# Batch 0's first stage in two tiles, filters released on half of x, and the last V/G weights behind D's first slab

## The chip, the cores and the metric

One NeuronCore of a Trainium2 chip runs the whole kernel. The metric is the device time of one execution in microseconds (us), median of several. Each kernel's time is compared with runs of the kernel before on its own chip and of its own rounds. Each trace is one execution, and most of the traces compared come from different chips. Times inside an execution count from the start of its span.

## The reference

```python
def _attn_ref(x, filt_r, filt_i):                    # x: 8 x 3008 x 256, f32
    X = np.fft.rfft(x, axis=1)
    Y = X * (filt_r + 1j * filt_i)[None]             # 1505 frequencies x 256
    return np.fft.irfft(Y, n=x.shape[1], axis=1)

def _moe_ref(x, w_gate, w_val, w_out):               # 24064 tokens, 256 -> 1536 -> 256
    return (np.maximum(x @ w_gate, 0.0) * (x @ w_val)) @ w_out
```

The kernel computes the second of the first. 3008 = 94 x 32, so the Fourier transform is done in stages: A (along the 94), B (forward along the 32, times the filter, and back), C (back along the 94, into y transposed), then the V, G and O matmuls on blocks of 512 tokens.

## The kernel before

Only batch 0 is exposed. The other seven batches' stages run between V/G/O matmuls. What follows is the start, cut to what the change touches; "..." marks cuts.

```python
XF = [pro.tile([128, NX2 * D], FP32, name=f"XF{c}") for c in range(N2 // NX2)]   # x, two halves
AS = pro.tile([128, NC2, N2 // NC2, D], BF16)        # stage A of batch 0
AT = pro.tile([128, 32, D], BF16)                    # the same, turned in 32 x 32 blocks
...
def first_a(p, s, h):                                # 16 of these; h is half of D
    ...
    nc.tensor.matmul(psA, WA[:, 0:128], xf[:, n:n + 4, h * D // 2:(h + 1) * D // 2], ...)
    nc.scalar.copy(AS[:, 4 * s:4 * s + 4, p, h * D // 2:(h + 1) * D // 2], psA)

def turn_a(h):
    src = AS.rearrange("p l c d -> p (l c) d").bitcast(FP32).rearrange("p n d -> p d n")
    dst = AT.bitcast(FP32).rearrange("p k d -> p d k")
    cols = slice(h * D // 4, (h + 1) * D // 4)
    nc.vector.transpose(dst[:, cols, :], src[:, cols, :])
...
load_own_filters()
hold_gpsimd(XF[1][:, 2 * q - 8:2 * q])     # GpSimd waits here for three quarters of x,
for _ in filters:                          # then issues the rest of the filters
    pass
...                                        # stage A on PE; filler matmuls; turns
place_filter(1, 1, 0, nc.scalar.copy)      # rows of the filters doubled: by ACT, by DVE,
place_filter(1, 0, 0, nc.vector.tensor_copy)
for half in range(2):                      # and by DMAs on SP's queue,
    for a in range(2):
        place_filter(0, a, half, nc.sync.dma_start)
load_x(1, nc.sync, ...)                    # behind which stands batch 1's x
...
def first_b(amid):
    for i in range(6):
        fwd(0, i)                          # PE: psX
        if i > 1:
            inv(0, i - 2, cuts=cuts)       # PE: psD; ACT: dsb; SP: Dbuf<-dsb
        for e in range(2):                 # DVE, or ACT copy + GpSimd, times the filters
            product(0, i, e, 0)
            product(0, i, e, 1, pool=(i, e) in POOL_U)
        amid(i)                            # stage A matmuls of batch 1 in between
...
def amid(i):
    ...
    if i in (2, 4):                        # third and fourth quarter of V and G
        load_vg((i + 2) // 2 * DFF // 4, (i + 4) // 2 * DFF // 4)
    for _ in range((1, 1, 1, 2, 1, 2, 1)[i]):
        next(early)()
hold_gpsimd(AT[0:32, NG - 1, D - 8:])
load_vg(0, DFF // 2)
first_b(amid)
load_d(0, 0, 2)                            # first two slabs of D, read on SP's queue
for i, f in enumerate(early):              # rest of batch 1's stage A
    f()
    if i == 5:
        item_c(0, 0); item_c(0, 1)         # PE: psY <- D, then yT
hold_gpsimd(yTs[0][:, 0, 0:8])
load_o()                                   # W_out
```

The engines in the profile: PE is TensorE (matmuls; PEld are its weight loads), DVE is VectorE, ACT is ScalarE, POOL is GpSimd, and SP is SyncE, which here only issues DMAs. An eviction copies a result out of PSUM, a turn is the transpose of one half of stage A in 32 x 32 blocks, a hold is a small copy that makes GpSimd wait for a tile, and a slab is a piece of D that is read back for stage C.

The names in the profile: `XF` (x), `psA` (stage A's result), `psX` (the forward transform), `Ftr`/`Fti` (the filters' real and imaginary parts), `psY` (stage C's result), `AS`, `AT`, `tt`/`uu` (products), `psD`/`dsb` (stage B's result and its eviction), `Dbuf` (D in HBM), `dC` (a slab of D read back), `asb`/`Abuf`/`at` (the same way for batch 1's stage A), `WvT`/`WgT`/`WoT` (weights).

Of the kernel before, what the change touches and what calls it, by code (L numbers as in the profile page):

```python
# [12 lines left out]
FP32 = mybir.dt.float32  # L13
BF16 = mybir.dt.bfloat16
# [15 lines left out]
N1, N2 = 94, 32  # L30
# [5 lines left out]
def _ap(t, offset_elems, ap_list):  # L36
    return dataclasses.replace(
        t, offset=t.offset + offset_elems, ap=[list(p) for p in ap_list]
    )
# [81 lines left out]
def kernel(  # L121
# [10 lines left out]
    nc = tc.nc  # L132
    B, S_, D = x.shape
    DFF = moe_w_gate.shape[1]
    NFT = DFF // 128
    assert S_ == S and D == 256 and DFF % 128 == 0
    NC2 = 8
# [14 lines left out]
    pro = prologue.enter_context(tc.tile_pool(name="pro", bufs=1))  # L152
# [3 lines left out]

    XF = [pro.tile([128, NX2 * D], FP32, name=f"XF{c}") for c in range(N2 // NX2)]
    WA = pro.tile([128, 128 + NROW], FP32)
    AS = pro.tile([128, NC2, N2 // NC2, D], BF16)
    AT = pro.tile([128, 32, D], BF16)  # L160
    WF = consts.tile([128, 4, 32], FP32)
    M1 = consts.tile([NROW, N1], BF16)
# [65 lines left out]
    def load_own_filters():  # L228
        for src, dst in FILT:
            nc.gpsimd.dma_start(dst[64:95:2, NG - 2:, :],  # L230
                                _ap(src, 47 * D, [[N1 * D, 16], [-47 * D, 2], [1, D]]))
            nyq.append(pro.tile([1, D], BF16, tag="nyq", bufs=2, name="nyq"))
            nc.gpsimd.dma_start(nyq[-1], _ap(src, (S // 2) * D, [[D, 1], [1, D]]))
# [8 lines left out]
    def place_nyq():  # L242
        for (src, dst), n in zip(FILT, nyq):
            nc.vector.tensor_copy(dst[96:97, NG - 1, :], n)

    def load_vg(c0, c1):
        for (w_hbm, w_sb) in ((moe_w_val, WvT), (moe_w_gate, WgT)):
            nc.gpsimd.dma_start(w_sb[:, :, c0:c1],
                                _ap(w_hbm, c0, [[DFF, 128], [128 * DFF, 2], [1, c1 - c0]]))
# [7 lines left out]
    def hold_gpsimd(tile_):  # L257

        scr = sb.tile([128, 8], FP32, tag="scr", bufs=2)
        nc.gpsimd.tensor_copy(scr[:tile_.shape[0]], tile_)  # L260
# [4 lines left out]
    def fft_tag(side=False):  # L265
        if side and turn.get("side"):
            return turn["side"]
        turn["i"] += 1
        return turn["tags"][turn["i"] % len(turn["tags"])]

    def first_a(p, s, h):

        psA = ps.tile([128, 4, D // 2], FP32, tag=fft_tag(True), name="psA")
        xf = XF[p // 2].rearrange("p (n d) -> p n d", d=D)
        n = p % 2 * NC2 + 4 * s
        nc.tensor.matmul(psA, WA[:, 0:128], xf[:, n:n + 4, h * D // 2:(h + 1) * D // 2],
                         start=True, stop=True)
        nc.scalar.copy(AS[:, 4 * s:4 * s + 4, p, h * D // 2:(h + 1) * D // 2], psA)

    def turn_a(h):  # L280

        src = AS.rearrange("p l c d -> p (l c) d").bitcast(FP32).rearrange("p n d -> p d n")
        dst = AT.bitcast(FP32).rearrange("p k d -> p d k")
        cols = slice(h * D // 4, (h + 1) * D // 4)
        nc.vector.transpose(dst[:, cols, :], src[:, cols, :])  # L285
        ats[0] = AT

    def items_a(b):
# [136 lines left out]
    def first_b(amid):  # L425

        cuts = (0, 2, 4, 5, 6)
        for i in range(6):
            fwd(0, i)
            if i > 1:  # L430
                inv(0, i - 2, cuts=cuts)
            for e in range(2):
                product(0, i, e, 0)
                product(0, i, e, 1, pool=(i, e) in POOL_U)
            amid(i)
        inv(0, 4, cuts=cuts)
        amid(6)
        inv(0, 5, cuts=cuts)

    dCs = {}  # L440

    def load_d(b, z0=0, z1=NZ):
        for z in range(z0, z1):
            dC = sb.tile([NROW, 8, D], BF16, tag="dC", bufs=6)
            for e in range(2):
                nc.sync.dma_start(dC[48 * e:48 * e + 48],
                                  _ap(Dbuf[b], (64 * e + 16 * z) * NG * D,
                                      [[D, 48], [48 * D, 8], [1, D]]))
            dCs[b, z] = dC
# [13 lines left out]
    def item_c(k, h):  # L463

        if h == 0:
            yTs[k] = sb.tile([128, 2, W], BF16, tag="yT", bufs=3, name="yT")
        tag = fft_tag() if k == 0 else ("psv", "psg")[h]
        psY = ps.tile([128, W], FP32, tag=tag, name="psY")
        for (o, b, n2, n1, w) in runs(k * W, W):
            nc.tensor.matmul(psY[:, o:o + w],  # L470
                             dCs[b, n2 // 8][:, n2 % 8, h * 128:(h + 1) * 128], M1[:, n1:n1 + w],
                             start=True, stop=True)
        dst = yTs[k][:, h]
        if h == 0:
            nc.scalar.copy(dst, psY)  # L475
        else:
            nc.vector.tensor_copy(dst, psY)
# [63 lines left out]
    q = NX2 * D // 4  # L541
# [13 lines left out]
    for (src, dst) in FILT:  # L555
        nc.vector.memset(dst[64:128, NG - 2:, :], 0.0)
    load_own_filters()
    hold_gpsimd(XF[1][:, 2 * q - 8:2 * q])
    for _ in filters:
        pass  # L560

# [4 lines left out]
    for s in range(2):  # L566
        for h in range(2):
            first_a(0, s, h)
    for i in range(3):
        make_back_u(i)  # L570
    for p, h in ((1, 0), (1, 1), (2, 0), (3, 0), (2, 1), (3, 1)):
        for s in range(2):
            first_a(p, s, h)
    place_own()
    for h in range(2):
        turn_a(h)
# [15 lines left out]
    def amid(i):  # L592
        if i == 3:
            place_nyq()
        if i in (2, 4):
            load_vg((i + 2) // 2 * DFF // 4, (i + 4) // 2 * DFF // 4)
        for _ in range((1, 1, 1, 2, 1, 2, 1)[i]):
            next(early)()

# [3 lines left out]
    first_b(amid)  # L603
    turn["tags"], turn["side"] = ("fft", "psv", "psg", "pso"), None
    load_d(0, 0, 2)
    for i, f in enumerate(early):
        f()
        if i == 5:
            for h in range(2):
                item_c(0, h)  # L610
# [21 lines left out]
    for b in range(1, B):  # L632
# [4 lines left out]
        else:  # L637
            for j, e in enumerate((-74, -69, -62, -55) if b == 2 else (-74, -69, -64, -57)):
                l = (22, 29, 34, 43)[j] if b == 2 else end - 115 + NFT * j
# [11 lines left out]
        for i in range(7):  # L651
            l = -35 + 5 * i if b == 1 else -40 + 6 * i
# [49 lines left out]
```

## Time and profile before

| | us |
|---|---|
| median before the change (first three runs, 896.4 to 898.69) | 896.96 |
| span of the profiled execution | 896.3 |
| first product of stage B starts | 32.82 |
| last eviction of stage B ends | 49.91 |
| D's last write lands | 55.46 |
| first psY of stage C starts | 60.15 |
| first V/G product on DVE | 64.91 |

The page gives busy us, share of the span and instructions of each engine, then the line of what the DMA engines moved in 40 slices of the span:

```profile
PE 874.9 (98%) x7186; PEld 507.2 (57%) x7186; DVE 572.8 (64%) x871; ACT 499.9 (56%) x889; POOL 364.6 (41%) x360
...
GB/s 222 275 242 97 128 134 162 102 109 116 136 150 129 99 126 123 142 138 98 99 161 135 109 102 95 191 124 93 108 141 154 117 32 82 74 82 36 37 29 54
```

PE has next to nothing to win after the start, and the DMA engines are busiest in the first three slices, 67 us. Landing times in this document come from the records of the sixteen completions of each transfer in the trace: a transfer has landed with its last one.

### The profile page before, as it was taken

To read this page: it belongs to the slowest core of one execution; us is meant where nothing else is said; L and a number is where in the kernel's file an instruction comes from. 1 tells how busy PE (TensorE), PEld (TensorE's weight loads), DVE (VectorE), ACT (ScalarE), POOL (GpSimd) and SP (SyncE) were. 2 spreads that over 40 slices of the span, in tenths; PEclk is the share of its full clock that TensorE was granted. 3 is DMA by queue.
4 is the path that set the end of the run, shared out by engine and by line. 5 is a ranking of instruction groups with operands and counts; after the bars stand their busy time and mean duration, and the time that the engine had idled before them with its cause. 6 is when DMAs were issued, how large, how long until landed. Compare 5 with 4: busy or idle time off the path is not lost.

```text
span 896.3 us, 19093 instructions
## 1 busy us (share of the span) xinstructions
PE 874.9 (98%) x7186; PEld 507.2 (57%) x7186; DVE 572.8 (64%) x871; ACT 499.9 (56%) x889; POOL 364.6 (41%) x360
## 2 busy tenths in 40 slices
PE   8779999999999999999999999999999999999998
PEld 3325555566556565566655665556655566666665
DVE  3827765577765776667766677656766577655554
ACT  5545655556555556555655565655555556555553
POOL 4431599028671386515673167811768000000001
PEclk9989999999999999999999999999999999999999
DMA  8994448444465344563365433753346512231111
GB/s 222 275 242 97 128 134 162 102 109 116 136 150 129 99 126 123 142 138 98 99 161 135 109 102 95 191 124 93 108 141 154 117 32 82 74 82 36 37 29 54
DMA packets 110769, 107.26 MB, mean 120 GB/s; under 512 B 20167, under 2 KB 95463, under 8 KB 110038
## 3 DMA queue, kind: packets, MB, share of 16 engines
q1 hardware_dynamic: 86998, 78.20, 34.1%
q0 software_dynamic: 22960, 26.40, 12.4%
q10 hardware_dynamic: 720, 1.45, 0.4%
q8 instruction: 56, 0.92, 0.4%
q14 instruction: 35, 0.29, 0.1%
HBM read 60.42 MB, written 48.23 MB: 121 GB/s over the span
## 4 chain that ended last, share of the span: by engine, by line
PE 90%; DMA 5%; DVE 2%; ACT 1%; SPq 1%; issue 1%; POOL 0%; DVEq 0%; POOLq 0%
PE psV L486 27%; PE psG L486 27%; PE psO L505 26%; PE psF L342 3%; PE psD L413 2%; PE psY L470 2%; PE psX L383 2%; DMA dC<-Dbuf 1%; PE psA L295 1%; DMA at<-Abuf 1%; DMA Ftr<-Ftr 1%; DMA Ftr<-in_filt_r_dram 1%; DMA Dbuf<-dsb 1%; DMA XF<-in_x_dram 1%; DVE AT L285 0%
## 5 line engine op out<-in xcount | busy, mean ns | idle before, releaser
L491 DVE SCALAR_TENSOR_TENSOR prod<-psG,vsb 128x512 bf16<-128x512 f32 x564 | 389.1, 690 | 265.2 <-ACT vsb L489 256.3
L489 ACT CAST vsb<-psV 128x512 bf16<-128x512 f32 x564 | 332.1, 589 | 262.7 <-PE psV L486 205.3
L486 PE MATMUL psV<-yT,WvT 128*128 128x512 bf16 x1128 | 336.9, 380 | 0.5 <-ACT asb L349 0.5
L505 PE MATMUL psO<-WoT,prod 128*128 128x256 bf16 x2256 | 336.4, 273 | 0.0
L486 PE MATMUL psG<-yT,WgT 128*128 128x512 bf16 x1128 | 335.3, 379 | 0.8 <-ACT dsb L420 0.3
L505 PEld LDWEIGHTS <-prod 128*128 128x128 bf16 x2256 | 220.5, 98 | 143.5
L486 PEld LDWEIGHTS <-WgT 128*128 128x128 bf16 x1128 | 110.1, 98 | 136.6 <-issue 3.8
L486 PEld LDWEIGHTS <-WvT 128*128 128x128 bf16 x1128 | 98.7, 98 | 42.0 <-issue 30.6
L260 POOL CAST scr<-prod 128x8 f32<-128x8 bf16 x24 | 4.6, 192 | 259.7 <-DVE prod L491 259.7
L528 POOL DMA_DIRECT2D out_dram<-osb x5 | 2.6, 535 | 195.9 <-ACT osb L518 195.9
L518 ACT COPY osb<-psO 128x512 f32<-128x512 f32 x92 | 53.9, 586 | 27.9 <-PE psO L505 26.8
L399 DVE TENSOR_TENSOR tt<-psX,Ftr 128x512 bf16<-128x512 f32 x96 | 65.2, 682 | 1.6 <-PE psX L383 1.6
L328 POOL TENSOR_TENSOR fold<-XP 128x1024 f32<-128x1024 f32 x24 | 56.6, 2356 | 20.9 <-PE psF L342 19.5
L399 DVE TENSOR_TENSOR uu<-psX,Fti 128x512 bf16<-128x512 f32 x89 | 60.6, 681 | 0.0
L420 ACT CAST dsb<-psD 128x512 bf16<-128x512 f32 x96 | 51.6, 589 | 13.1 <-PE psD L413 13.1
L315 POOL DMA_DIRECT2D XP<-in_x_dram x96 | 56.7, 596 | 3.1 <-PE psY L470 1.5
L329 POOL TENSOR_TENSOR XP<-XP 128x1024 f32<-128x1024 f32 x24 | 56.4, 2350 | 1.9
L470 PE MATMUL psY<-M,dC 96*128 96x94 bf16 (+18 forms) x604 | 38.1, 200 | 8.0 <-DMA dC<-Dbuf 7.8
L475 ACT CAST yT<-psY 128x512 bf16<-128x512 f32 x47 | 27.6, 586 | 30.6 <-PE psY L470 30.4
L349 ACT CAST asb<-psF 128x512 bf16<-128x512 f32 x48 | 25.8, 589 | 30.5 <-PE psF L342 30.5
L349 DVE CAST asb<-psF 128x512 bf16<-128x512 f32 x48 | 30.9, 686 | 18.6 <-PE psF L342 18.6
L470 PEld LDWEIGHTS <-dC 96*128 96x128 bf16 x604 | 34.8, 98 | 12.5 <-issue 8.3
(75 smaller groups left out, 490.4 us busy)
## 6 DMA issues: line engine op xcount, KB each, us to landing
dC<-Dbuf SPq DMA_DIRECT2D x64, 192.0 KB
XP<-in_x_dram POOLq DMA_DIRECT2D x48, 256.0 KB, 6.0
Dbuf<-dsb SPq DMA_DIRECT2D x23, 512.0 KB
at<-Abuf SPq DMA_DIRECT2D x28, 384.0 KB
XP<-in_x_dram POOLq DMA_DIRECT2D x96, 96.0 KB, 2.7
Abuf<-asb SPq DMA_DIRECT2D x96, 96.0 KB
out_dram<-osb SPq DMA_DIRECT2D x69, 94.0 KB
XF<-in_x_dram SPq DMA_DIRECT2D x15, 256.0 KB
```

The lines of the kernel that those rows point to most:

```text
L315: nc.gpsimd.dma_start(xp[r:r + 24, 0:4:2, :], _ap(x, (b * N1 * N2 + o) * D, [[N2 * D, 24], [47 * N2 * D, 2], [1, 512]]))
L328: tt(t, xp[:, 0:2], xp[:, 2:4], op=ALU.add)
L329: tt(xp[:, 2:4], xp[:, 0:2], xp[:, 2:4], op=ALU.subtract)
L349: copy(asf[:, :, q, :], banks[q])
L399: nc.vector.tensor_tensor(p, psX, filt, op=ALU.mult)
L420: nc.scalar.copy(dsb[:, a, o:o + 2, :], psD[a])
L470: nc.tensor.matmul(psY[:, o:o + w], dCs[b, n2 // 8][:, n2 % 8, h * 128:(h + 1) * 128], M1[:, n1:n1 + w], start=True, stop=True)
L486: nc.tensor.matmul(pt[:, :W], w[:, h, ft * 128:(ft + 1) * 128], yt[:, h, :], start=(h == 0), stop=(h == 1))
L489: nc.scalar.copy(vsb, psV[:, :W])
L491: nc.vector.scalar_tensor_tensor(prod, in0=psG[:, :W], scalar=0.0, in1=vsb, op0=ALU.max, op1=ALU.mult)
L505: nc.tensor.matmul(psO[:, t % 2], prods[ft][:, t * 128:(t + 1) * 128], WoT[:, ft, :], start=(ft == 0), stop=(ft == NFT - 1))
L518: copy(osb[:, t0 % 2:t % 2 + 1], psO[:, t0 % 2:t % 2 + 1])
```

## The change

The intent has three parts. Part 1 keeps the two halves of batch 0's stage A in a tile each, so that each half can be turned when its own eight evictions are done. Part 2 lets GpSimd issue the filters when half of x is there, not three quarters. Part 3 takes the last two quarters of V and G (called the quarters below) out of stage B and issues them when D's first slab has landed.

```diff
-    AS = pro.tile([128, NC2, N2 // NC2, D], BF16)
+    AS = [pro.tile([128, NC2, N2 // NC2, D // 2], BF16, name=f"AS{h}") for h in range(2)]
...
-        nc.scalar.copy(AS[:, 4 * s:4 * s + 4, p, h * D // 2:(h + 1) * D // 2], psA)
+        nc.scalar.copy(AS[h][:, 4 * s:4 * s + 4, p, :], psA)
...
-        src = AS.rearrange("p l c d -> p (l c) d").bitcast(FP32).rearrange("p n d -> p d n")
+        src = AS[h].rearrange("p l c d -> p (l c) d").bitcast(FP32).rearrange("p n d -> p d n")
...
-        nc.vector.transpose(dst[:, cols, :], src[:, cols, :])
+        nc.vector.transpose(dst[:, h * D // 4:(h + 1) * D // 4, :], src)
...
-    hold_gpsimd(XF[1][:, 2 * q - 8:2 * q])
+    hold_gpsimd(XF[0][:, 4 * q - 8:4 * q])
...
-        if i in (2, 4):
-            load_vg((i + 2) // 2 * DFF // 4, (i + 4) // 2 * DFF // 4)
...
     load_d(0, 0, 2)
+    hold_gpsimd(dCs[0, 0][:, 7, D - 8:])
+    for c in range(2, 4):
+        load_vg(c * DFF // 4, (c + 1) * DFF // 4)
```

More of the change, by code (lines that the diff above doesn't have):

```diff
@@ L277, in first_a @@
                          start=True, stop=True)
-        nc.scalar.copy(AS[:, 4 * s:4 * s + 4, p, h * D // 2:(h + 1) * D // 2], psA)
+        nc.scalar.copy(AS[h][:, 4 * s:4 * s + 4, p, :], psA)
     def turn_a(h):
-        src = AS.rearrange("p l c d -> p (l c) d").bitcast(FP32).rearrange("p n d -> p d n")
+        src = AS[h].rearrange("p l c d -> p (l c) d").bitcast(FP32).rearrange("p n d -> p d n")
         dst = AT.bitcast(FP32).rearrange("p k d -> p d k")
-        cols = slice(h * D // 4, (h + 1) * D // 4)
-        nc.vector.transpose(dst[:, cols, :], src[:, cols, :])
+        nc.vector.transpose(dst[:, h * D // 4:(h + 1) * D // 4, :], src)
         ats[0] = AT
```

## The prediction

> **What bounds the kernel now.** I read the page first, then the chain of waits, then the timelines of the start, then the DMA queues in stretches of 2 us. The page has PE busy 98% of the span, and the chain that ends last is 90% PE. After about 75 us the chain is an unbroken run of V, G and O matmuls, which the change does not touch. So only what lies before the first V matmul (62.79 us) can move the end, and each us gained there should come off the end. The chain of the start, in order of time (start, length, what):
>
> ```profile
> 27.75 4.06 DVE AT L285
> 31.84 0.96 DVE Fti L240
> 32.84 0.68 DVE tt L399
> ...
> 49.93 5.53 DMA Dbuf<-dsb
> ...
> 59.06 5.86 DMA at<-Abuf
> ```
>
> Three pieces are to be seen: turns of AT ahead of the first product, a 5.5 us wait for D's last write, then reads. The timelines (start, length, engine, line, operation, and in brackets the idle time before it) show why:
>
> ```profile
> 19.51 0.59 ACT L278 CAST AS<-psA 128x512 bf16<-128x512 f32 x1 [0.27 <-PE psA L276]
> ...
> 22.94 0.59 ACT L278 CAST AS<-psA 128x512 bf16<-128x512 f32 x1 [0.27 <-PE psA L276]
> 28.48 2.75 ACT L240 COPY Fti<-Fti 32x3072 bf16<-32x3072 bf16 x1 [4.95 <-DMA Fti<-in_filt_i_dram]
> ```
> ```profile
> 23.56 8.25 DVE L285 STREAM_TRANSPOSE AT<-AS 128x2048 f32<-128x2048 f32 x2 [10.21 <-ACT AS L278]
> 31.84 0.95 DVE L240 COPY Fti<-Fti 32x3072 bf16<-32x3072 bf16 x1
> 32.82 0.69 DVE L399 TENSOR_TENSOR tt<-psX,Ftr 128x512 bf16<-128x512 f32 x1
> ```
> ```profile
> 14.50 0.19 POOL L260 COPY scr<-XF 128x8 f32<-128x8 f32 x1 [6.14 <-DMA XF<-in_x_dram]
> 14.99 0.61 POOL L225 DMA_DIRECT2D Ftr<-in_filt_r_dram  x1 [0.30 <-issue]
> ```
> ```profile
> 60.15 1.01 PE L470 MATMUL psY<-M,dC 96*128 96x94 bf16 x12 [6.08 <-DMA dC<-Dbuf]
> ```
>
> DVE has stood idle 10.21 us when both turns run, and they start only after the sixteenth eviction (22.94 + 0.59). In the program order the last eviction of half 0 is the eighth of the last twelve, the one at 19.51. PE later waits 6.08 us for D's first slab. The stretches (PE, weight loads, DVE, ACT, POOL busy; then granted clock, DMA share, GB/s):
>
> ```profile
> 14.00:16.00 2.00, 2.00 (x6) 0.88 (x5) 0.00 (x0) 1.26 (x3) 1.20 (x3) 1.00 0.56 234
> 30.00:32.00 2.00, 0.14 (x5) 0.14 (x8) 1.97 (x2) 1.23 (x1) 0.12 (x1) 1.00 1.08 368
> 34.00:36.00 2.00, 2.00 (x10) 0.44 (x10) 1.90 (x4) 1.26 (x3) 0.82 (x2) 0.50 1.00 307
> 50.00:52.00 2.00, 2.00 (x6) 0.81 (x5) 0.00 (x0) 1.45 (x3) 0.00 (x0) 1.00 1.17 295
> 60.00:62.00 2.00, 1.85 (x14) 1.31 (x15) 0.69 (x1) 0.59 (x1) 0.58 (x2) 0.50 1.19 260
> ```
>
> DMA is full from 16 to 54 us but for one hole at 14 to 16. The clock is halved after each PE gap.
>
> **What the Trainium skill says.** "DMA: Bandwidth & Descriptors", section "Queues, rings and completion order": each DMA engine takes turns between the queues it has work for, packet by packet. The trace agrees: at 44 to 46 us the hardware queue took 61.4% and the software queue 55.8%. So weights issued by GpSimd delay D's writes. The same page, "Anatomy of one DMA — SWDGE (gpsimd) path", fits a transfer as about 2.0 us plus its bytes; the trace shows 3.6 us at the least from issue to landing of a filter piece and 10.2 us for the last, which queue. "TensorE: Matmul & The Clock Gate", "What's actually happening": a free-running window of 3413 ns, and an idle window halves the clock. The trace agrees: 0.50 at 34 to 36 us after a gap of 3.78 us, and at 58 to 62 us.
>
> **Part 1, two AS tiles.** The instruction order is the same on every engine; only the waits of the two turns differ (each now has its own). Turn 0 can start at 19.51 + 0.59 + 0.03 = 20.13 us. A turn takes 8.25 / 2 = 4.12, so it ends at 24.25. Half 1 is written by 23.53, so turn 1 runs 24.25 to 28.37. Then the DVE filter copy, 0.95, and the first product at 29.36 in place of 32.82: **3.46 us** on the path, if the filters are there.
>
> **Part 2, filters held for half of x.** The first product also needs Ftr's first-half copies (landed 27.59 by the completion records, so no bound on 29.36), and the next one the ACT copy of Fti, which ended at 28.48 + 2.75 = 31.23. Without part 2 that would take back 1.3 us. XF[0] landed at 12.23, the old hold's piece at 14.34: the issue moves 2.11 us earlier, from 14.99 to 12.88. First packets came 1.4 us after the issue, so now at 14.3. x has then about 0.8 us of packets left, which half rate stretches to 1.6, to land near 17.0 in place of 16.17. PE wants that piece at 12.37 + 6 x 0.86 = 17.5, so stage A is not delayed. The filters gain 2.1 less about 0.8 of sharing: 1.3 us. Fti lands at 27.1, and ACT ends at 29.9; the second product wants it at 29.97. Parts 1 and 2 fit within 0.1 us. Batch 1's first x, which landed at 31.19, comes at 29.9, and PE wants it at 28.8: a stall of 1 us that hides beside DVE.
>
> Stage B itself (32.82 to its last eviction at 48.84 + 1.07 = 49.91, 17.1 us) should shrink too. PE's gap before it falls from 3.78 us to 0.3, so the half clock at 33.0 to 36.4 should go; DVE idled 0.70, 0.31 and 0.87 us for PE there. POOL loses four weight issues (0.75, 0.71, 0.75, 0.71) that stood between its products. ACT, busy 13.6 of those 15.2 us from its first copy, is the floor. I take **1.0 us**, a choice, so B's last eviction is at 49.91 - 3.46 - 1.0 = 45.4.
>
> **Part 3, last V/G quarters after D's slab.** It removes 0.79 MB of weights (as written) from beside D's writes. Work on the DMA engines, as share times length of the 2 us stretches by queue: filters 9.4 us, hardware queue to 42 us 14.2, first V/G half 4.5, last quarters 5.4, then D and A writes 7.2 + 1.1. That is 41.8 in the 39 us from 16.4 to 55.4, a capacity of 1.07. Without the last quarters and half of the last A write it is 35.9, so 33.5 us, and from 15.3 (the hole filled) it ends at 48.8. The engines' own path gives 45.4 plus about 4 (the first D slab took 3.1 us from issue to landing with few others about), so 49.4. The two limits are close and will rub; I take 50.0 for D's last write in place of 55.46: **5.5 us**, which contains all of the gains above (3.5 + 1.0 + about 1.0 of a shorter write). The read of the first slab takes 4.5 us as before (55.55 to 60.02), so it lands at D = 54.5.
>
> The cost: the quarters now go behind D. Hold and first issue at D + 0.6, first packets at about D + 2.4. The remaining reads (half of slab 1, A of batch 1) have then some 3.4 us of work; two pieces of c=2 are 2.7 us. Taking turns, they end at D + 7.2 and land by D + 7.7; c=3 lands near D + 10.5; W_out (5 us of work) at D + 13 and D + 16. Before, V started 2.77 us after the slab, reached feature block 6 at D + 8.7, block 9 at D + 11.7, and O at D + 15.8 and 17.1. All have about 1 us to spare. I allow **0.6 us** of stall on average. The half clock after D's wait may give back some: one window rather than two would be worth 0.6, not sure because the window runs free. Sum: 5.5 - 0.6 + 0.4 = **5.3 us**.
>
> **Rivals.** (a) Weights late: the last quarters miss block 6 or 9 by 2 to 4 us, or W_out misses O. For it: earlier quarters took 6.4 to 10.1 us from issue, and 8 us is all there is; against it: the reads beside them end soon. Time 893.5 to 896. (b) Early filters slow x: XF[1] lands after 17.5 and stage A loses up to 2 us, or Fti still lands at 28.4 because DMA is full, so the second product waits on ACT as before. For it: shares of 1.0 to 1.2; against: the idle hole. Time 892.5 to 894. (c) DMA is not what D's write waits for, its own latency is, and the gain is parts 1 and 2 alone: 3.5 us, 893.5. (d) Everything fits and both half-clock windows vanish: 889.
>
> **Range and chances.** 896.96 - 5.3 = **891.7 us**. (a) to (c) pull up, (d) down; runs spread about 1 us. So 889.2 to 895.0. The whole stretch at stake is 62.8 us with at most some 8 us to win, and 2% is 17.9 us: faster by over 2% 0.01, within 2% 0.98, slower 0.01.
>
> **What would show it.** The first turn at 20.1 and first product near 29.4; ACT's Fti copy near 27; clock 1.00 at 29 to 36; D's last write landing near 50 and the first psY near 54.6; no PE gap over 0.5 us in V/G of block 0 (a gap ended by WvT or WgT means rival a). If the first product comes at 29.4 and psY less than 4 us earlier, the DMA sum was wrong. A change that showed only after 75 us would refute the whole reading.

## The result

| | before | changed |
|---|---|---|
| median, us (4 runs each) | 897.83 (896.4 to 899.18) | 891.36 (891.01 to 893.75) |
| ratio | | 0.9934, 95% interval 0.9909 to 0.9959 |
| span of the profiled execution | 896.3 | 889.2 |

A ratio is the mean time of one kernel's fast runs over the mean of the other's of the same rounds, so not quite the ratio of the medians. 1 - 0.9934 is 5.9 us of 897.8. By the 2% mark this is "same", and it is clear of noise.

The timelines of the changed kernel: first DVE, ACT and GpSimd, then PE (start, us, engine, line, operation, and in brackets the idle time before it and what ended it). Lines of the source are one lower than before.

```profile
20.12 8.29 DVE L284 STREAM_TRANSPOSE AT<-AS 128x2048 f32<-128x2048 f32 x2 [6.19 <-ACT AS L278]
28.45 0.95 DVE L240 COPY Fti<-Fti 32x3072 bf16<-32x3072 bf16 x1
29.43 0.69 DVE L398 TENSOR_TENSOR tt<-psX,Ftr 128x512 bf16<-128x512 f32 x1
```
```profile
24.89 2.75 ACT L240 COPY Fti<-Fti 32x3072 bf16<-32x3072 bf16 x1 [1.36 <-DMA Fti<-in_filt_i_dram]
```
```profile
12.01 0.19 POOL L260 COPY scr<-XF 128x8 f32<-128x8 f32 x1 [3.63 <-DMA XF<-in_x_dram]
```
```profile
54.66 0.62 PE L469 MATMUL psY<-M,dC 96*128 96x94 bf16 x12 [3.97 <-DMA dC<-Dbuf]
```

Turn 0 starts at 20.12 in place of 23.56 and the first product at 29.43 in place of 32.82. Stage C's first psY starts at 54.66 in place of 60.15. The chain that ended last, at stage B's end (start, us, what), and the stretches (PE, weight loads, DVE, ACT, POOL busy, clock, DMA share, GB/s):

```profile
45.45 1.07 ACT dsb L419 x2
46.52 0.02 ACT asb L297
46.54 2.43 DMA Dbuf<-dsb
...
49.44 5.09 DMA dC<-Dbuf
```
```profile
32.00:34.00 2.00, 1.06 (x15) 0.59 (x15) 1.71 (x3) 2.00 (x5) 1.98 (x2) 1.00 1.01 353
34.00:36.00 2.00, 1.34 (x17) 0.43 (x19) 1.19 (x2) 1.82 (x4) 1.99 (x3) 1.00 0.95 334
```

D's last write takes 2.43 us where it took 5.53, the slab's read takes longer than before (5.46 us in place of 4.47, by the completions), and the clock is whole at 34 to 36 us. The first V/G product on DVE comes at 59.27, 5.64 us earlier. The distance between the two traces stays 5.64 us, product by product, until block 4. There PE of the kernel before waited once more, 1.8 us for a slab of batch 1's D, and the profiled spans end 7.1 us apart. In the fourteen profiles that wait was 2.0 us in e2, 1.8 in this one, 1.5 in e1 and 0 to 0.5 in the others. All three are kernels with the quarters inside stage B, but two more of that kind (e5, e9) did not have it, so whether the change has a part in it is not shown. What is read below is the 5.64 us of the start.

### The profile page after: what moved, and what is told of

It is laid out like the page before. It is cut to its first block, busy times and chain, and to the rows that moved or that the text cites. A ratio compares the mean times of both kernels' runs of the same rounds, so it can differ in the third digit from the quotient of the medians.

```text
span 889.2 us, 18975 instructions
## 1 busy us (share of the span) xinstructions
PE 866.7 (97%) x7065; PEld 506.8 (57%) x7186; DVE 572.9 (64%) x871; ACT 500.0 (56%) x889; POOL 365.3 (41%) x361
## 4 chain that ended last, share of the span: by engine, by line
PE 86%; DVE 4%; ACT 4%; DMA 3%; issue 2%; POOL 0%; SPq 0%; DVEq 0%; POOLq 0%; ACTq 0%
PE psG L485 27%; PE psO L504 25%; PE psV L485 25%; DVE prod L490 3%; PE psF L341 3%; ACT vsb L488 3%; PE psD L412 2%; PE psX L382 2%; PE psY L469 2%; DMA Ftr<-Ftr 1%; DMA Ftr<-in_filt_r_dram 1%; PE psA L294 1%; DMA dC<-Dbuf 1%; DMA XF<-in_x_dram 1%; ACT dsb L419 0%
## 5 line engine op out<-in xcount | busy, mean ns | idle before, releaser
L485 PE MATMUL psG<-yT,WgT 128*128 128x512 bf16 x1107 | 331.0, 379 | 6.9 <-DVE prod L490 0.8
L485 PE MATMUL psV<-yT,WvT 128*128 128x512 bf16 x1030 | 315.8, 380 | 0.5 <-ACT asb L348 0.5
L517 ACT COPY osb<-psO 128x512 f32<-128x512 f32 x92 | 54.0, 586 | 27.9 <-PE psO L504 26.5
L476 DVE CAST yT<-psY 128x512 bf16<-128x512 f32 x47 | 32.0, 681 | 11.6 <-PE psY L469 11.6
```

Source lines behind the costliest of these rows:

```text
L485: nc.tensor.matmul(pt[:, :W], w[:, h, ft * 128:(ft + 1) * 128], yt[:, h, :], start=(h == 0), stop=(h == 1))
L517: copy(osb[:, t0 % 2:t % 2 + 1], psO[:, t0 % 2:t % 2 + 1])
```

## The experiments

Twelve runs were made, one of them of the changed kernel again, all with correct results (the labels e7 and e10 are not on record). These times (us) are from the profiled execution of each; "PE waits" is PE's wait for batch 1's x inside stage B, "lag" runs from the end of stage B's last eviction to the landing of D's last write, "slab read" from the first read's issue to the landing of the second half of the first slab.

| kernel | Fti copy on ACT starts | first product | PE waits | stage B | last eviction | lag | slab read | first psY |
|---|---|---|---|---|---|---|---|---|
| before | 28.48 | 32.82 | - | 17.09 | 49.91 | 5.55 | 4.47 | 60.15 |
| changed | 24.89 | 29.43 | 0.16 | 17.09 | 46.52 | 2.46 | 5.46 | 54.66 |
| e1_tiles_only | 28.61 | 29.61 | 4.06 | 20.57 | 50.18 | 6.26 | 3.80 | 60.45 |
| e2_hold_only | 25.52 | 32.73 | - | 17.28 | 50.01 | 5.23 | 3.73 | 59.19 |
| e3_weights_only | 26.74 | 32.36 | - | 17.27 | 49.63 | 2.45 | 5.58 | 57.88 |
| e4_old_hold | 27.66 | 29.28 | 3.03 | 20.06 | 49.34 | 2.43 | 5.58 | 57.58 |
| e5_warm_only | 27.79 | 32.52 | - | 17.09 | 49.61 | 5.37 | 3.97 | 59.17 |
| e6_a_write_behind_d | 26.19 | 29.35 | 1.03 | 17.09 | 46.44 | 3.07 | 3.67 | 53.40 |
| e8_copy_first | 25.17 | 29.12 | 0.69 | 20.77 | 49.89 | 2.44 | 5.65 | 58.20 |
| e9_weights_back | 28.57 | 29.60 | 2.06 | 19.14 | 48.74 | 5.42 | 3.69 | 58.06 |
| e11_changed_again | 27.66 | 29.39 | 2.19 | 20.37 | 49.76 | 2.44 | 5.50 | 57.92 |
| e12_both_moved | 24.90 | 29.16 | 0.37 | 17.09 | 46.25 | 2.48 | 3.97 | 52.91 |
| e13_at_behind_w | 26.87 | 29.17 | 1.58 | 17.52 | 46.69 | 2.44 | 5.53 | 54.88 |
| e14_later_item | 25.18 | 29.00 | 0.40 | 17.21 | 46.21 | 2.65 | 3.74 | 52.82 |

Each row is one execution. That of the changed kernel was the fastest of its four; those of e1, e4 and e11 were the slowest of theirs, so rows next to each other differ by luck as well as by edit.

The theory going in: the start is a serial chain, and the total of DMA work bounds D's write. The rival for the second half: D's write follows the engines by a fixed delay.

### One part at a time

**e1_tiles_only**: the kernel before with the AS hunks alone.

```diff
-    AS = pro.tile([128, NC2, N2 // NC2, D], BF16)
+    AS = [pro.tile([128, NC2, N2 // NC2, D // 2], BF16, name=f"AS{h}") for h in range(2)]
...
```

> Only the two stage-A tiles (part 1), added to the kernel before. Theory (serial chain, DMA total bounds D's write): first turn at 20.1 us, first product at 29.4, but the second product waits for the ACT copy of Fti until about 31.3, so stage B's last eviction ends near 47.8 (before 49.9, changed kernel 46.5); D's last write still lands at 54.5 to 55.4 because the same bytes are queued in the DMA engines, so psY gains only 0 to 1 us and the time is 0 to 1 us under before. Rival (D's write follows the engines by a fixed delay): D lands 5.5 us after the last eviction, near 53.3, and the time is about 2.2 us under before.

Ratio 0.9988, interval 0.9954 to 1.0022: no gain shown. The first turn came at 19.72 and the second product at 31.39, as expected. But stage B took 20.57 us, so its last eviction was even later than before. Both theories missed that. PE's timeline shows the wait:

```profile
28.16 0.41 PE L382 MATMUL psX<-AT,F 64*64 64x256 bf16 x8 [0.48 <-DVE AT L284]
32.63 1.39 PE L294 MATMUL psA<-XF,WA 128*96 128x512 f32 x2 [4.06 <-DMA XF<-in_x_dram]
```

PE kept to the program's order: the second forward product started at 34.02 us, behind that matmul. It is a stage A matmul of batch 1, recorded behind the first forward product, and that x is read on SP's queue behind the copies of the filters. Turning earlier alone brings PE to that matmul before its data: SP issued the read that PE waited for at 26.87, where it does so at 23.36 in the changed kernel.

**e2_hold_only**: the kernel before with the hold's hunk alone.

```diff
-    hold_gpsimd(XF[1][:, 2 * q - 8:2 * q])
+    hold_gpsimd(XF[0][:, 4 * q - 8:4 * q])
```

> Only the earlier filter hold (part 2), added to the kernel before. Theory: Fti lands near 25 us in place of 28.4 as in the changed kernel, the first product stays at 32.8 because both turns still wait for the sixteenth eviction, and the last eviction stays at 49.9; the DMA queue is 1 to 2 us ahead, so D's last write may land 1.0 to 1.5 us earlier: gain 0 to 1.5 us. Rival (D's write follows the engines by a fixed delay): no gain at all, 0.0 us.

Fti came at 25.52, and first product and last eviction did not move. D's write landed at 55.24, 0.22 us earlier: the fixed delay, not the DMA total. psY was 0.96 us earlier, all but 0.22 of it from a shorter slab read. The timing was poor (ratio 1.0033, interval 0.998 to 1.0086, one run of 905.37), so no gain and no loss can be claimed.

**e3_weights_only**: the kernel before with part 3's hunks alone.

```diff
-        if i in (2, 4):
-            load_vg((i + 2) // 2 * DFF // 4, (i + 4) // 2 * DFF // 4)
...
+    hold_gpsimd(dCs[0, 0][:, 7, D - 8:])
+    for c in range(2, 4):
+        load_vg(c * DFF // 4, (c + 1) * DFF // 4)
```

> Only the last V/G quarters behind D's first slab (part 3), added to the kernel before. Theory: start unchanged (first product 32.8, last eviction 49.9), D's last write lands some 2.5 to 3 us after the last eviction, near 52.5 in place of 55.5; the slab read is 1 us longer (5.5 in place of 4.5) as the A write issued by ACT now falls into it; psY near 58.1 in place of 60.2, gain about 2 us. Rival (DMA total is the bound of the whole stage): removing 5.4 us of DMA work brings D's write forward by up to 5 us and more than half of the change's gain appears here, over 3.5 us.

The lag fell to 2.45 us, the slab read rose to 5.58, and psY came at 57.88: the theory's numbers within 0.5. In the chain of waits, D's last write:

```profile
49.66 2.42 DMA Dbuf<-dsb
```

Ratio 0.9977, interval 0.9945 to 1.0008: about the 2 us expected, but not clear of noise. The run does not decide against the DMA total by itself, since stage B's end would have held D's write back under either theory.

**e4_old_hold**: the changed kernel with the old hold, parts 1 and 3.

```diff
-    hold_gpsimd(XF[0][:, 4 * q - 8:4 * q])
+    hold_gpsimd(XF[1][:, 2 * q - 8:2 * q])
```

> The changed kernel with the old, later filter hold (parts 1 and 3). Theory: first product at 29.4, second waits for the ACT copy of Fti, done at 31.2; last eviction 47.8 in place of 46.5, and psY and the time 1.3 us above the changed kernel. Rival: the filters were never needed earlier, or what stage B loses at its start is hidden later: time equal to the changed kernel within 0.3 us.

Ratio 0.9963, interval 0.9931 to 0.9996. The last eviction was at 49.34, so 2.8 us were lost against the changed kernel's trace where 1.3 were expected (the times, 0.9963 and 0.9934, have overlapping intervals), and not through ACT's copy (the second product waited for it only 0.47 us). It was batch 1's x again:

```profile
31.76 1.07 PE L294 MATMUL psA<-XF,WA 128*96 128x512 f32 x2 [3.03 <-DMA XF<-in_x_dram]
```

**e9_weights_back**: parts 1 and 2, the last quarters back inside stage B (the hunks of part 3 undone).

```diff
+        if i in (2, 4):
+            load_vg((i + 2) // 2 * DFF // 4, (i + 4) // 2 * DFF // 4)
...
-    hold_gpsimd(dCs[0, 0][:, 7, D - 8:])
-    for c in range(2, 4):
-        load_vg(c * DFF // 4, (c + 1) * DFF // 4)
```

> The changed kernel with the last V/G quarters back inside stage B (parts 1 and 2). Theory (DMA total): last eviction near 46.5 to 47.5 as in the changed kernel, but D's last write lands near 53.5 to 54.5, 7 us behind it, as weights and writes take turns; psY near 58.5; time 1.2 to 2.0 us under before, so part 3 is worth some 4 us beside the others where alone it gave 2.3. Rival (fixed delay of 5.5 us behind the last eviction): D lands at 52, psY near 56.5, time 3.5 us under before.

Ratio 0.9948, interval 0.9933 to 0.9963. D landed at 54.16, inside the theory's range, but for the rival's reason: the last eviction was late (48.74, since filters and x were late in this execution) and the lag was 5.42:

```profile
48.77 5.39 DMA Dbuf<-dsb
```

So this run alone does not separate the two; the table's column speaks for the fixed delay. With the quarters inside stage B the lag is 5.23 to 6.26 in five kernels, without them 2.43 to 3.07 in nine, wherever stage B ended between 46.2 and 50.2. e2 is the sharpest of them: its filters landed 3 us earlier than before and D's write only 0.22. So the DMA total up to there was not the bound, and part 3 takes about 3 us off the lag. Not all of it is kept. From the end of stage B to psY, the five kernels with the quarters inside took 9.2 to 10.3 us (mean 9.7), and the six without them that leave the third A write where it was took 8.1 to 8.3 (mean 8.2), because their slab read is longer. Part 3 is worth about 1.5 us at psY. By the times (0.9948 here, 0.9934 and 0.9935 for the changed kernel) it is 1.2 us, within the noise.

### The clock and stage B

**e5_warm_only**: the kernel before with 16 more filler matmuls ahead of stage B.

```diff
     for i in range(12):
-        warm(2)
+        warm(3 + (i % 3 == 0))
```

> The kernel before, with 16 more filler matmuls in front of stage B so that PE does not stand still for 3.8 us there. Theory now (the PE clock was not what set stage B's length): the granted clock is 1.00 at 33 to 36 us, and stage B from its first product to the end of its last eviction still takes 17.1 us, within 0.3. Rival (the term in the prediction): with the clock whole, stage B shrinks by 0.7 to 1.0 us.

One execution, 897.92. The clock was whole:

```profile
32.00:34.00 2.00, 2.00 (x12) 0.54 (x12) 1.97 (x4) 0.00 (x0) 1.94 (x3) 1.00 1.07 230
34.00:36.00 2.00, 1.12 (x14) 0.37 (x14) 2.00 (x4) 1.56 (x4) 0.89 (x1) 1.00 0.97 340
```

Stage B still took 17.09 us, to the hundredth what the kernel before took with half the clock at 34 to 36. The half clock stood beside DVE and ACT work and cost nothing in stage B.

**e8_copy_first**: the changed kernel; for products that ACT and GpSimd share, ACT's copy is recorded ahead of DVE's product.

```diff
             for e in range(2):
-                product(0, i, e, 0)
-                product(0, i, e, 1, pool=(i, e) in POOL_U)
+                pool = (i, e) in POOL_U
+                for k in ((1, 0) if pool else (0, 1)):
+                    product(0, i, e, k, pool=pool and k == 1)
```

> The changed kernel, with ACT's copy for a GpSimd product recorded ahead of the DVE product of the same psX, so that ACT's chain starts at about 29 us in place of 31.35. Theory (stage B's length is set by ACT and GpSimd, which start late behind DVE): stage B from first product to last eviction takes 15.5 to 16.4 us in place of 17.1, and psY starts 0.7 to 1.6 us earlier. Rival (PE's in-order mix of batch 1 matmuls, or DVE, sets it): 16.8 to 17.4 us, no gain.

Ratio 0.9963, interval 0.9947 to 0.998. ACT did start at 28.66, but stage B took 20.77 us: neither theory. DVE now waits for ACT's copies, which stand behind ACT's evictions:

```profile
34.12 1.29 DVE L398 TENSOR_TENSOR tt<-psX,Ftr 128x512 bf16<-128x512 f32 x2 [1.36 <-ACT xs L395]
...
40.54 1.29 DVE L398 TENSOR_TENSOR tt<-psX,Ftr 128x512 bf16<-128x512 f32 x2 [1.49 <-ACT xs L395]
```

So an earlier start of ACT did not shorten stage B, but the edit brought in new waits of DVE, so it is no clean test of what ACT's late start costs. What sets 17.09 us stays open.

### The slab read and the weights behind it

**e6_a_write_behind_d**: the changed kernel; batch 1's third A write issued by SP, behind the slab reads.

```diff
-                eng = nc.scalar if c > 1 else nc.sync
+                eng = nc.scalar if c > 2 else nc.sync
```

> The changed kernel, with the third write of batch 1's A issued by SP behind the reads of D's first two slabs, not by ACT before them. Theory (that write took turns with the slab read): the read of D's first slab takes 4.3 to 4.6 us from first issue to last landing in place of 5.5, psY starts about 1.0 us earlier, time about 0.7 to 1.0 us under the changed kernel's 891.2. Rival (the read is slower because its latency or the HBM is, whatever runs beside): read 5.2 to 5.6 us and time as the changed kernel, or worse, because A's read then waits for A's write.

The slab read fell to 3.67 us, below the 4.3 to 4.6 of the theory, and psY came 1.26 us earlier:

```profile
53.40 0.62 PE L469 MATMUL psY<-M,dC 96*128 96x94 bf16 x12 [2.79 <-DMA dC<-Dbuf]
```

So that write, in flight until 52.47 in the changed kernel's trace, was what made the read longer; D's earlier landing had moved the read onto it. But the time did not follow (ratio 0.9958, interval 0.9931 to 0.9984). PE waited for weights:

```profile
62.84 0.61 PE L485 MATMUL psG<-yT,WgT 128*128 128x512 bf16 x2 [1.26 <-DMA WgT<-in_moe_w_gate_dram]
...
73.02 0.38 PE L504 MATMUL psO<-WoT,prod 128*128 128x256 bf16 x2 [1.66 <-DMA WoT<-in_moe_w_out_dram]
```

V's third quarter landed at 60.92 where it landed at 60.79 in the changed kernel, although issued 1.26 us earlier. This is the prediction's rival (a), brought out by a faster slab.

**e11_changed_again**, the changed kernel itself, ran on the chip of the next two.

> The changed kernel itself, once more, on the chip of the next two runs. Both theories: about 0.993 to 0.995 of before; stage B 17.1 us from first product to last eviction, D's last write 2.4 to 3.1 us behind the last eviction, no gap of PE in block 0 over 0.5 us. Spread from the filters' landing (24.8 to 28.5 us in the runs so far) moves all of it by up to 2 us.

Median 892.79 (six runs, 890.83 to 895.52), ratio 0.9935, interval 0.9919 to 0.995, as in the first measurement. Its profiled execution was the slowest of the six: Fti landed late, PE waited 2.19 us for batch 1's x, and stage B took 20.37 us, against the 17.1 expected. Part 2 does not always keep x from being late: SP issued the read that PE waited for at 23.85, only 0.5 us later than in the first trace of the changed kernel, and its first completion came at 27.45 in both, but its last came at 30.94 in place of 28.95. The clock was halved around that wait:

```profile
32.00:34.00 2.00, 2.00 (x11) 0.58 (x10) 0.37 (x1) 0.93 (x2) 1.15 (x1) 0.50 1.00 267
34.00:36.00 2.00, 2.00 (x14) 0.46 (x16) 0.92 (x2) 1.59 (x3) 0.98 (x1) 0.50 1.14 368
```

**e12_both_moved**: e6's edit, and the three first reads of batch 1's A behind W_out in GpSimd's queue (the fourth stays on SP's, recorded at the same place).

```diff
-        nc.sync.dma_start(ats[b][c:c + 125:4],
+        eng = nc.gpsimd if c < 3 else nc.sync
+        eng.dma_start(ats[b][c:c + 125:4],
...
     load_o()
+    for c in range(4):
+        load_at(1, c)
...
-            for c in range(4):
-                at_step(c, lambda c=c: load_at(1, c))
+            pass
```

> The changed kernel with the third A write behind the slab reads, and the three first reads of batch 1's A moved into GpSimd's queue behind W_out. Theory (the weights' slack is a matter of who takes turns with them; with A's reads gone from beside them they land in time): slab read about 3.7 us in place of 5.5, psY 1.2 to 1.8 us earlier than in the changed kernel relative to the last eviction, gaps of PE for V, G and W_out under 0.5 us in sum, time 0.7 to 1.5 us under the changed kernel. Rival (the DMA total up to 73 us is the bound, the order only says who waits): the gaps return as weight waits or as a wait for A's read before batch 1's first forward product near 75 us; time as the changed kernel or above.

Median 891.41 (889.26 to 892.55), ratio 0.9919, interval 0.9905 to 0.9932. Over the same rounds its mean is 891.19, e11's is 893.01: 1.8 us less, but the two intervals overlap (0.9919 to 0.9932), so the gain is likely and not clear of noise. psY came at 52.91 and PE waited for no weight; of A's reads it waited 0.40 us for one. In its trace the clock stayed whole past D's wait, which was 2.50 us:

```profile
52.91 0.62 PE L470 MATMUL psY<-M,dC 96*128 96x94 bf16 x12 [2.50 <-DMA dC<-Dbuf]
```

**e13_at_behind_w**: the edit of A's reads alone, on the changed kernel (the last three hunks above).

> The changed kernel with the three reads of batch 1's A behind W_out alone (third A write stays on ACT). Theory: the last V/G quarters land 1 to 2 us earlier after D's slab than in the changed kernel (there 6.3 and 7.3 us for c=2, 10.0 and 10.3 for c=3), the slab read stays at 5.5 us, and the time stays as the changed kernel's within 0.5 us, since the weights did not hold PE up there. Rival: A's reads come too late for batch 1 and the time rises by 1 us or more.

Median 893.03, ratio 0.9933, interval 0.992 to 0.9946: as e11. The third quarters landed 4.2 and 7.2 us behind the slab in place of 6.3 and 7.3. Alone, that edit shows no gain.

**e14_later_item**: e12, with batch 1's first two matmuls one step later.

```diff
-        for _ in range((1, 1, 1, 2, 1, 2, 1)[i]):
+        for _ in range((0, 1, 2, 2, 1, 2, 1)[i]):
```

> The version with A's third write and A's reads moved (e12), and batch 1's first stage-A matmul recorded one step later in stage B, behind the second forward product. Theory (late filters lengthen stage B only because PE, in order, stands at batch 1's x in front of the second forward product): stage B takes 17.1 to 17.5 us whatever the landing of the filters and of x, and the runs spread less; ratio to before 0.989 to 0.992. Rival (late x costs the same wherever the matmul stands, or the moved matmul delays A's writes): stage B 18 us or more when x lands after 30 us, ratio 0.992 or above.

Ratio 0.9936, interval 0.9921 to 0.995, on another chip. In its profile x had landed by 29.03, so the case that it was made for did not arise; the ratio is on the rival's side. It shows no gain over e12 and does not tell the theories apart.

## Why the prediction was right

The time, 891.36, is 0.3 us from the predicted 891.7, and inside the range. Part 1's mechanism was right, and so was the step of part 3 that weights beside D's writes delay them. Three terms of the sum were nevertheless wrong, stage B's length, D's write and the slab's read, and that they cancel is luck.

- **Part 1** held within 0.1 us: first turn 20.12 (predicted 20.13), first product 29.43 (29.36).
- **Part 2** was near in size, and incomplete in what it is for. Fti's copy starts at 26.1 on average over the nine profiles with the new hold (24.89 to 28.57) and at 27.9 over the five with the old one (26.74 to 28.61): 1.7 us, where 1.3 was predicted. In the profiled run it was 3.6. x's last piece landed at 17.27 (17.0 predicted). But in the traces its main worth is not ACT's copy. It is batch 1's x, which stands behind the filters' copies on SP's queue. The prediction had this wait as "a stall of 1 us that hides beside DVE". It does hide at 1.03 us (e6, stage B 17.09); at 1.58 it costs 0.4, at 2.06 to 4.06 it costs 2.1 to 3.5 (in e1 and e9 the second product also waited 1.1 us for ACT's copy). PE's wait was 3.03 and 4.06 us in the two profiles with part 1 and the old hold, and 0.16 to 2.19 in the eight with both parts. Without part 2, no gain of part 1 is shown: e1 shows no change, e4 is hardly better than e3 at psY (57.58, 57.88). How much of the loss is the wait and how much the half clock that follows it was not separated.
- **Stage B's 1.0 us** was wrong: 17.09 us before and after. e5 takes away the half clock alone and finds it free; e3 takes away GpSimd's four weight issues and stays at 17.27. ACT, called the floor, was busy 12.9 of the 15.2 us by its records, not 13.6.
- **D's write** was predicted at 50.0, from the "capacity of 1.07" of the DMA engines, and landed at 48.98. The sum of DMA work was the wrong bound. The lag behind the last eviction, 5.55 before and 2.46 after, went with whether the quarters are in the way and with nothing else that was tried. The sum took share times length as work, but in the stretches of the kernel before a share of 0.91 moved 124 GB/s (20 to 22 us) and one of 1.08 moved 361 (52 to 54 us), so a share near 1 is not a fixed rate of bytes. That this is why the sum misled is not shown.
- **The slab's read** was predicted "as before", 4.5 us, and took 5.46, because the third A write now falls into it (e6: 3.67 without). These three terms, +1.1 at the last eviction, -2.1 on the write and +1.0 on the read, cancel, so that psY came at 54.66 against 54.6.
- **The weights** landed in time: the third quarters 6.3 and 7.3 us behind the slab, the fourth 10.0 and 10.3, W_out 12.3 and 14.7. The 0.6 us allowed for a stall was not needed, but e6 shows that the slack was about as thin as said: there a slab 1.3 us earlier, with A's reads later and so beside the weights, brings the stalls out. The half clock behind D's wait fell from two windows to one.
- **The total.** 5.3 predicted; 5.6 at the first V/G product of the two traces; 5.9 by the ratio. The gain of one execution depends on when filters and x land: in e11's trace only 2.2 us were gained at the first V/G product. That the chain after 75 us is unbroken did not hold for the kernel before, which waited 1.8 us in block 4.

The three parts together moved psY by 5.5 us in the profiled run, while e1, e2 and e3 alone moved it by -0.3, 1.0 and 2.3. That is 2.5 us more than their sum, but single executions vary by up to 3 us here. The waits in e1 and e4 offer a reason, that part 1 brings nothing until part 2 removes what PE meets next; the times are too noisy to show it.

## What to carry to other kernels

- When a wait is shortened, look at the next instruction in the order of every engine that is released earlier, and ask when its data lands. Here a PE wait that hid beside DVE at 1 us no longer did at 2.
- Try to take weight loads out from beside the last write that a stage ends with, and look what else runs beside the read that follows, since it moves into a new neighbourhood: here half of the 3 us won on the write was lost on the read.
- A half clock in the profile need not cost anything; fill the gap once and measure the stage.
- Note whether a profiled execution was among the fast or the slow ones of its kernel before reading a difference of 2 us from it.

## What the Trainium skill lacked or had wrong

- "TensorE: Matmul & The Clock Gate", section "What's actually happening", agrees with the traces in window length (3.41 us in the clock records). It has the clock halve after an idle window, and the prediction took it so; here the window did not have to be idle. Cut into such windows, the fourteen traces have 19 halvings. They followed windows in which PE, by its records, was busy 0.00 to 1.41 of the 3.41 us (1.15 us before the halving at 33.0 in the kernel before); after every window of whole clock with 1.59 us or more the clock stayed whole. So waits of 2.06 (e9) and 2.19 us (e11) went with a halving and waits of 2.50 (e12) and 2.79 (e6) did not. The ends of matmuls are modelled, so these figures are approximate. The page's advice is to avoid such gaps; it gives no way to tell when the penalty is on the path. Here a half-clock window of 3.4 us over PE's work cost 0.00 us of stage B (17.09 with and without).
- "DMA: Bandwidth & Descriptors", section "Queues, rings and completion order", has the engines take turns. It does not say what this does to the landing of a small last write: 2.4 to 3.1 us behind its data without the quarters, 5.2 to 6.3 beside their 0.79 MB of weight loads (as written).
- The same page, section "Anatomy of one DMA — SWDGE (gpsimd) path": by its fit a filter piece that reads 384 KB (192 KB as written) would take an estimated 2.9 us (2.0 + 0.9). The quickest in the trace of the kernel before took 3.7 (issued at 14.99, landed at 18.64). Other transfers ran beside it (DMA share 0.56 at 14 to 16 us), so this does not show the fit wrong for a transfer alone.
- No page gives a number for how far apart the sixteen completions of one transfer can lie. For the last filter piece it was 22.18 to 24.80 us in the changed kernel and 22.52 to 28.48 in e9. A wide spread went with a late start of V and G: the first V/G product came at 59.27 us in the changed kernel's first trace and at 62.67 in e11, where the piece's completions ran from 22.13 to 27.58.
